# Head mixing on parts of TensorE's array: premix on quarters, mix on row halves, ten tokens gathered to partitions 4 to 123

## The chip, the cores and the metric

One core of one Trainium2 chip runs the whole kernel. The metric is device time in microseconds, the median of repeated runs. The core's engines are TensorE (PE in the profile, its weight loads are PEld), VectorE (DVE), ScalarE (ACT), GpSimd (POOL) and SyncE (SP), which here only issues transfers. SBUF is the on-chip memory of 128 partitions, PSUM holds what TensorE writes, in banks of 512 float32 per partition.

## The reference

Attention whose heads are mixed before and after the softmax ("talking heads"), followed by a gated feed-forward layer. B = 8, H = 12 heads, S = 448 tokens, D = 64; the model width is 768, the hidden width 2048, all float32.

```python
scores = scale * q @ k.transpose(0, 1, 3, 2)
scores = einsum('bhij,hg->bgij', scores, w_pre)      # "premix" over heads
scores = scores - max(scores, axis=-1)
attn = exp(scores)
attn = attn / (sum(attn, axis=-1) + 1e-9)
attn = einsum('bhij,hg->bgij', attn, w_post)         # "mix" over heads
x = (attn @ v) as (B * S, 768)
h = x @ w_in
out = (h - tanh(h)) @ w_out
```

## The kernel before

The kernel has a short prologue, an attention loop over 180 places, and a feed-forward part (from line 865 on) that the change doesn't touch.

**Blocks and groups.** The queries of a batch are cut into blocks of 120, 120, 120 and 88 tokens, 32 blocks in all. `scores` (line 465) computes a pair of heads of one block: three products of the split operands (float32r, high and low parts) on each row half of the array, as D = 64 fills half of its rows. The results land in `sts`, with a query token on each partition. A group is ten tokens of a block (nine in the last ones); `gather` (line 492) brings its 10 x 12 rows (token, head) by one transfer to 120 partitions of a tile `t`, so that mixing over heads is a product with a 120 x 120 matrix: `wpre` is block diagonal, with `w_pre` repeated for each of the ten tokens, and `wpost` holds `w_post` in an order that sorts the result by head, then token. There are 360 groups, and place p handles groups 2p and 2p + 1.

**A place** (lines 817 to 860). The order of instructions on each engine is the order in which they are written; `in_order` at the end pins it. In place p stand, one after another:

1. the copy of the previous mix result from PSUM to `at` (line 565, ScalarE),
2. the gathers for groups 2p + 4 and 2p + 5 and up to six other transfers, on SP's queue,
3. `premix(p)` (line 507): the even group as one float32 product; the odd group as three float32r products of `wph`, `wpl` (the split of `wpre`) with `th`, `tl`,
4. `norm(p - 1)`: the reciprocal of the softmax sums (VectorE) and the scaling of `wpost` by them into `wr` (line 544, ScalarE),
5. `split(2p + 3)` (line 498): the high part `th` on VectorE (line 503), the low part `tl` on GpSimd (line 504),
6. `expo(p)`: for each of the two groups the row maximum (line 526, VectorE) and the exponential with its sum (line 528, ScalarE),
7. jobs that a planner spreads over the places: transposes of k (line 415) and q (line 441), `values` (line 585, the product with v on column halves of the array, with lines 597 and 615), `scores` of a later block; their copies from PSUM follow,
8. `mix(p - 1)` (line 547): for each of the two groups and each of four chunks of 112 keys one float32 product, with the exponentials as weights (112 columns) and `wr` (120 columns) as the moving operand,
9. a step of the conversion of the feed-forward weights (lines 71 to 110, on VectorE, ScalarE and GpSimd).

The PSUM tiles are two for premix (`ps_p`), one pair of banks for mix (`ps_o`) and four for the jobs (`ps_m`). The gather tiles are two rings, of three for even groups and two for odd ones. In the prologue `wpre` and `wpost` are built from w_pre and w_post by a product with a selection matrix, copies, and selects on GpSimd that cut the block diagonal (lines 674 to 695). A float32 product shows as two records in TensorE's rows, a float32r product as one.

Of the kernel before, what the change touches and what calls it, by code (L numbers as in the profile page):

```python
# [21 lines left out]
def raw(ap):  # L22

    return ap.bitcast(F32)
# [124 lines left out]
def kernel_body(  # L149
# [11 lines left out]
    nc = tc.nc  # L161
    B, H, S, D = q.shape
    P = 128
# [3 lines left out]
    CP = 112  # L167
    NC = S // CP
    GI = P // H
    MT = GI * H  # L170
    GP = GI * H
    starts = list(range(0, S, MT))
    sizes = [min(MT, S - s) for s in starts]
    NM = len(sizes)
    scale = 1.0 / float(D) ** 0.5
# [161 lines left out]
    with ExitStack() as st:  # L337
# [17 lines left out]
        kks, vts, krs, qrs, qbs, sts, ats = {}, {}, {}, {}, {}, {}, {}  # L355
# [131 lines left out]
        tokens = {t: range(g, sizes[blocks[i][1]], ngs[blocks[i][1]]) for t, (i, g) in enumerate(groups)}  # L487
        rows = {t: H * len(x) for t, x in tokens.items()}
        at_of = {t: sum(rows[u] for u in range(t - g, t)) // H for t, (i, g) in enumerate(groups)}
        tg, ts, te = {}, {}, {}  # L490

        def gather(t, eng=nc.sync):
            i, g = groups[t]
            x = gp.tile([GP, S], F32, name="t", tag=f"t{t % 2}", bufs=3 - t % 2)
            eng.dma_start(x[: rows[t], :], sts[i][tokens[t].start : tokens[t].stop : tokens[t].step])
            tg[t] = x

        def split(t, eng=nc.gpsimd):
            n = rows[t]
            x = tg.pop(t)  # L500
            th = gp.tile([GP, S], F32R, name="th", tag="th", bufs=2)
            tl = gp.tile([GP, S], F32R, name="tl", tag="tl", bufs=2)
            nc.vector.tensor_copy(th[:n, :], x[:n, :])  # L503
            eng.tensor_sub(tl[:n, :], x[:n, :], raw(th[:n, :]))  # L504
            ts[t] = (th, tl)

        def premix(p):

            pa, pb = [ps_p.tile([P, S], F32, name="ps_p", tag="ps_p") for _ in range(2)]
            n = rows[2 * p]  # L510
            nc.tensor.matmul(pa[:n, :], wpre[:n, :n], tg.pop(2 * p)[:n, :], start=True, stop=True)  # L511
            n = rows[2 * p + 1]
            th, tl = ts.pop(2 * p + 1)
            nc.tensor.matmul(pb[:n, :], wph[:n, :n], th[:n, :], start=True, stop=False)  # L514
            nc.tensor.matmul(pb[:n, :], wpl[:n, :n], th[:n, :], start=False, stop=False)  # L515
            nc.tensor.matmul(pb[:n, :], wph[:n, :n], tl[:n, :], start=False, stop=True)  # L516
            return pa, pb

        def expo(p, pss):
            zs = gp.tile([GP, 3, 2], F32, name="zs", tag="zs")  # L520
            es = []
            for j, ps in enumerate(pss):
                n = rows[2 * p + j]

                mx = gp.tile([GP, 1], F32, name="mx", tag="mx")
                nc.vector.tensor_reduce(out=mx[:n, :], in_=ps[:n, :], axis=AX.X, op=ALU.max, negate=True)  # L526
                e = gp.tile([GP, S], F32, name="e", tag="e", bufs=4)
                nc.scalar.activation(  # L528
                    e[:n, :], ps[:n, :], AF.Exp, bias=mx[:n, :], scale=1.0, accum_out=zs[:n, 0, j : j + 1]
                )  # L530
                es.append(e)
            te[p] = [es, zs]

        def norm(p):
            zs = te[p][1]
            wr = gp.tile([GP, 2, P], F32, name="wr", tag="wr", bufs=2)[:, :, :GP]
            n0, n1 = rows[2 * p], rows[2 * p + 1]
            for j, n in enumerate((n0, n1)):

                nc.vector.tensor_scalar_add(zs[:n, 1, j : j + 1], zs[:n, 0, j : j + 1], 1e-9)  # L540
            for js, n in ((slice(0, 2), n0),) if n0 == n1 else ((slice(0, 1), n0), (slice(1, 2), n1)):
                nc.vector.reciprocal(zs[:n, 2, js], zs[:n, 1, js])
            for j, n in enumerate((n0, n1)):
                nc.scalar.mul(wr[:n, j, :], wpost[:n, :], zs[:n, 2, j : j + 1])  # L544
            te[p].append(wr)

        def mix(p):
            es, _, wr = te.pop(p)
            ps = ps_o.tile([P, 2, 512], F32, name="ps_o", tag="ps_o")
            for j, e in enumerate(es):  # L550
                i, g = groups[2 * p + j]
                n = rows[2 * p + j]
                if g == 0:
                    ats[i] = kp.tile([CP, NC, H, MT], F32, name="at", tag="at", bufs=2)
                for c in range(NC):
                    nc.tensor.matmul(  # L556
                        ps[:CP, j, c * GP : (c + 1) * GP], e[:n, c * CP : (c + 1) * CP], wr[:n, j, :],
                        start=True, stop=True,
                    )

            def rest():
                (i0, _), (i1, _) = groups[2 * p], groups[2 * p + 1]
                n0, n1, at = rows[2 * p] // H, rows[2 * p + 1] // H, at_of[2 * p]
                if i0 == i1 and n0 == n1 == GI:
                    nc.scalar.copy(  # L565
                        ats[i0][:, :, :, at : at + 2 * GI].rearrange("p c h (j i) -> p j (c h) i", j=2),
                        ps[:CP, :, : NC * GP].rearrange("p j (x i) -> p j x i", i=GI),
                    )
                    return
                for j, (i, n) in enumerate(((i0, n0), (i1, n1))):  # L570
                    at = at_of[2 * p + j]
                    nc.scalar.copy(
                        ats[i][:, :, :, at : at + n],
                        ps[:CP, j, : NC * GP].rearrange("p (c h i) -> p c h i", c=NC, i=GI)[:, :, :, :n],
                    )

            return rest
# [69 lines left out]
        now()  # L647
        load_q(2)
        now()
        tmp_w = kp.tile([P, 2 * GP + 2 * H], F32, name="tmp_w", tag="at", bufs=2)  # L650
        w12 = tmp_w[:H, 2 * GP : 2 * GP + 2 * H].rearrange("p (w h) -> p w h", w=2)
        nc.scalar.dma_start(w12[:, 0, :], w_pre)
        nc.scalar.dma_start(w12[:, 1, :], w_post)

# [5 lines left out]
        def bank():  # L660
            return ps_p.tile([P, S], F32, name="ps_p", tag="ps_p")

        def scores_of(i, hq):
# [7 lines left out]
        prep_q(0, 1)  # L671
        flush()

        repeat = tmp_w[:H, GP : 2 * GP]
        nc.gpsimd.memset(repeat, 0.0)
        nc.gpsimd.affine_select(
            out=repeat.rearrange("p (i h) -> p i h", i=GI), in_=repeat.rearrange("p (i h) -> p i h", i=GI),
            compare_op=ALU.not_equal, fill=1.0, base=0, pattern=[[0, GI], [-1, H]], channel_multiplier=1,
        )
        ps_w = bank()[:GP, : 2 * H].rearrange("p (w g) -> p w g", w=2)  # L680
        nc.tensor.matmul(ps_w.rearrange("p w g -> p (w g)"), repeat, w12.rearrange("p w g -> p (w g)"), start=True, stop=True)
        wpre, wpost = [cst.tile([GP, P], F32, name=x)[:, :GP] for x in ("wpre", "wpost")]
        pre_v = wpre.rearrange("p (i g) -> p i g", i=GI)
        post_v = wpost.rearrange("p (g i) -> p g i", i=GI)
        nc.vector.tensor_copy(pre_v, ps_w[:, 0, :].unsqueeze(1).to_broadcast([GP, GI, H]))
        nc.vector.tensor_copy(post_v, ps_w[:, 1, :].unsqueeze(2).to_broadcast([GP, H, GI]))
        for x, step in ((pre_v, [[H, GI], [0, H]]), (post_v, [[0, H], [H, GI]])):

            nc.gpsimd.affine_select(
                out=x, in_=x, compare_op=ALU.is_ge, fill=0.0, base=0, pattern=[[-a, n] for a, n in step],  # L690
                channel_multiplier=1,
            )
            nc.gpsimd.affine_select(
                out=x, in_=x, compare_op=ALU.is_ge, fill=0.0, base=H - 1, pattern=step, channel_multiplier=-1,
            )


        busy(3, ps_b)
# [17 lines left out]
        prep_q(1, 0)  # L716
        prep_q(1, 1)
        flush()
        wph, wpl = [cst.tile([GP, P], F32R, name=x)[:, :GP] for x in ("wph", "wpl")]
        nc.vector.tensor_copy(wph, wpre)  # L720
        nc.vector.tensor_sub(wpl, wpre, raw(wph))

        NG = len(groups)
        for t in range(4):
            gather(t, (nc.sync, nc.scalar)[t % 2])
        place[0] += 1
        scores_of(1, 0)
        split(1, nc.vector)
        NPL = NG // 2
        conv = Steps(narrow_steps(nc, cv, partial(dma, to=slow), chunks), 11 * len(chunks) + 1, NPL - 16)  # L730

# [85 lines left out]
        for p in range(NPL + 3):  # L817
# [15 lines left out]
            if p == NPL:  # L833
                for f in x0[1:]:
                    f()
            if p + 1 < NPL:
                split(2 * p + 3)
            if p < NPL:
                expo(p, ps)
            for f, *a in todo[p]:  # L840
# [94 lines left out]
```

## Time and profile before

| what | value |
|---|---|
| median of 3 runs | 1862.28 us (1861.75 to 1863.77) |
| the profiled execution | 1859.88 us, its span 1858.2 us |
| attention loop | 24.5 to 914 us of the span |
| TensorE busy | 1844.0 us, 99% of the span |
| VectorE, ScalarE, GpSimd busy | 1230.1, 1099.2, 455.4 us |
| granted TensorE clock | 1.00 |

The span runs from the first to the last instruction; the execution's own time is 1.7 us more. A row of a group of instructions gives the line, the engine, the operation, the tiles (out<-in) with partitions x elements, the count, the busy time and the mean duration of one; behind the bar the idle time before them and what ended it. Rows of TensorE such as 120*112 120x120 give rows*columns of the weights and the moving operand. Matmuls are pipelined: a record lasts longer than the step from one to the next.

### The profile page before, as it was taken

The page shows a single profiled execution, that of the slowest core. Times are in us where ns is not written, and L with a number is a line of the kernel's source. Part 1 is how long each engine was busy: PE and PEld are TensorE (multiplying, and loading weights), DVE is VectorE, ACT ScalarE, POOL GpSimd, SP SyncE. Part 2 cuts the span into 40 slices and gives each one's busy share as a digit, 9 for nine tenths or more (in the row PEclk, how much of TensorE's full clock was granted, in tenths as well). Part 3 has the DMA queues.
Part 4 walks back from the last instruction along what each step waited for, and adds up shares of the span by engine and source line. Part 5 has one row for each costly group of instructions (what it writes and reads, how often), then busy time and mean ns, then how long its engine had stood idle before and what let it go on. Part 6 is the DMA issues. An engine that isn't in the chain of part 4 may idle for free.

```text
span 1858.2 us, 35351 instructions
## 1 busy us (share of the span) xinstructions
PE 1844.0 (99%) x13150; PEld 1523.0 (82%) x13150; DVE 1230.1 (66%) x2549; ACT 1099.2 (59%) x2411; POOL 455.4 (25%) x401
## 2 busy tenths in 40 slices
PE   8999999999999999999999999999999999999998
PEld 6888788788888888887788888888888888888887
DVE  5787777877787777776456556565565556556555
ACT  5877878788787887877633434434444443443433
POOL 2444445444444445444200000000000000000000
PEclk9999999999999999999999999999999999999999
DMA  8668576675765758554575665655656655655651
GB/s 179 189 185 217 167 204 197 195 220 172 225 188 169 229 180 229 178 176 151 194 297 198 224 219 196 236 202 209 231 197 218 223 207 209 218 219 194 225 202 37
DMA packets 232795, 371.92 MB, mean 200 GB/s; under 512 B 98992, under 2 KB 207536, under 8 KB 218288
## 3 DMA queue, kind: packets, MB, share of 16 engines
q1 hardware_dynamic: 231740, 368.45, 61.1%
q8 instruction: 104, 1.70, 0.4%
q10 hardware_dynamic: 884, 1.22, 0.2%
q14 instruction: 67, 0.55, 0.1%
HBM read 245.37 MB, written 47.19 MB: 157 GB/s over the span
## 4 chain that ended last, share of the span: by engine, by line
PE 95%; DMA 2%; ACT 1%; DVE 1%; issue 1%; POOL 0%; SPq 0%; ACTq 0%; POOLq 0%
PE ps_o L556 17%; PE ps_m L597 8%; PE ps_h L256 8%; PE ps_h L260 8%; PE ps_h L255 8%; PE ps_p L511 7%; PE ps_q L475 7%; PE ya L303 5%; PE ya L300 5%; PE ya L301 5%; PE yb L303 3%; PE yb L301 3%; PE yb L300 3%; PE ps_p L516 2%; PE ps_p L514 2%; PE ps_p L515 2%
## 5 line engine op out<-in xcount | busy, mean ns | idle before, releaser
L556 PEld LDWEIGHTS ps_o<-wr,e 120*112 120x112 f32 (+1 forms) x2880 | 307.2, 177 | 45.9 <-issue 29.0
L556 PE MATMUL ps_o<-wr,e 120*112 120x120 f32 (+1 forms) x2880 | 340.0, 271 | 1.6 <-ACT wr L544 1.6
L504 POOL TENSOR_TENSOR tl<-t,th 120x448 fp32r<-120x448 f32 x179 | 204.6, 1143 | 378.9 <-DVE th L503 194.0
L287 ACT CAST gh<-r 128x512 fp32r<-128x512 f32 x112 | 69.6, 621 | 374.4 <-DVE r L280 374.4
L526 DVE TENSOR_REDUCE mx<-ps_p 120x1 f32<-120x448 f32 x360 | 217.7, 621 | 105.9 <-PE ps_p L511 105.6
L256 PE MATMUL ps_h<-xl,w 128*128 128x512 f32 x672 | 263.2, 392 | 0.5 <-POOL pad L222 0.5
L255 PE MATMUL ps_h<-xh,w 128*128 128x512 f32 x672 | 262.8, 391 | 0.0
L528 ACT ACTIVATE e<-ps_p,mx 120x448 f32<-120x448 f32 x360 | 225.0, 631 | 27.9 <-DVE mx L526 26.9
L245 POOL TENSOR_TENSOR xl<-rx,xh 128x512 fp32r<-128x512 f32 x38 | 56.2, 1479 | 738.7 <-ACT xh L244 723.1
L565 ACT COPY at<-ps_o 112x960 f32<-112x960 f32 x156 | 153.6, 985 | 134.1 <-PE ps_o L556 133.0
L276 DVE SCALAR_TENSOR_TENSOR r<-qa,ps_h 128x512 f32<-128x512 f32 x112 | 77.0, 688 | 158.7 <-ACT t L273 158.7
L303 PE MATMUL ya<-w,gl 128*128 128x512 f32 x448 | 176.8, 395 | 0.7 <-DVE gl L288 0.7
L300 PE MATMUL ya<-w,gh 128*128 128x512 f32 x448 | 174.9, 390 | 1.9 <-ACT gh L287 1.9
L301 PE MATMUL ya<-w,gh 128*128 128x512 f32 x448 | 174.8, 390 | 0.0
L260 PE MATMUL ps_h<-xh,w 128*128 128x512 f32 x672 | 170.5, 389 | 0.0
L511 PE MATMUL ps_p<-t,wpre 120*120 120x448 f32 x360 | 165.3, 541 | 1.7 <-ACT e L528 0.9
L597 PE MATMUL ps_m<-at,vr 112*64 112x120 f32 (+1 forms) x3072 | 161.1, 261 | 0.0
L597 PEld LDWEIGHTS ps_m<-at,vr 112*64 112x64 f32 x3072 | 147.6, 137 | 12.9 <-issue 3.3
L270 ACT ACTIVATE u<-ps_h 128x512 f32<-128x512 f32 x112 | 66.9, 597 | 149.9 <-PE ps_h L260 149.9
L260 PEld LDWEIGHTS ps_h<-xh,w 128*128 128x128 f32 x672 | 126.1, 188 | 26.2
L256 PEld LDWEIGHTS ps_h<-xl,w 128*128 128x128 f32 x672 | 126.6, 188 | 24.6 <-POOL pad L222 0.9
L255 PEld LDWEIGHTS ps_h<-xh,w 128*128 128x128 f32 x672 | 126.6, 188 | 22.9
(102 smaller groups left out, 3623.9 us busy)
## 6 DMA issues: line engine op xcount, KB each, us to landing
w<-ws SPq DMA_DIRECT2D x112, 1536.0 KB
t<-s SPq DMA_DIRECT2D x342, 210.0 KB
cr<-in_moe_w_in_dram SPq DMA_DIRECT2D x24, 512.0 KB
cr<-in_moe_w_out_dram SPq DMA_DIRECT2D x32, 384.0 KB
vr<-in_v_dram SPq DMA_DIRECT2D x24, 448.0 KB
kr<-in_k_dram SPq DMA_DIRECT2D x23, 448.0 KB
out_dram<-ob SPq DMA_DIRECT2D x24, 384.0 KB
qr<-in_q_dram SPq DMA_DIRECT2D x23, 360.0 KB
```

What stands on the lines that cost most here:

```text
L255: nc.tensor.matmul(ph, wh[:, fs], xh, start=(c == 0), stop=False)
L256: nc.tensor.matmul(ph, wh[:, fs], xl, start=False, stop=False)
L260: nc.tensor.matmul(ph, wl[:, fs], xh, start=False, stop=(c == NK - 1))
L300: nc.tensor.matmul(y, gh[:, tok], wh[:, es], start=first, stop=False)
L301: nc.tensor.matmul(y, gh[:, tok], wl[:, es], start=False, stop=False)
L303: nc.tensor.matmul(y, gl[:, tok], wh[:, es], start=False, stop=last)
L504: eng.tensor_sub(tl[:n, :], x[:n, :], raw(th[:n, :]))
L511: nc.tensor.matmul(pa[:n, :], wpre[:n, :n], tg.pop(2 * p)[:n, :], start=True, stop=True)
L526: nc.vector.tensor_reduce(out=mx[:n, :], in_=ps[:n, :], axis=AX.X, op=ALU.max, negate=True)
L528: nc.scalar.activation(e[:n, :], ps[:n, :], AF.Exp, bias=mx[:n, :], scale=1.0, accum_out=zs[:n, 0, j : j + 1])
L556: nc.tensor.matmul(ps[:CP, j, c * GP : (c + 1) * GP], e[:n, c * CP : (c + 1) * CP], wr[:n, j, :], start=True, stop=True,)
L597: nc.tensor.matmul(pv[j * D : (j + 1) * D, r, :n], vt[:, j, c, :], ats[i][:, c, 2 * hp + j, :n], start=(c == 0), stop=(c == NC - 1),)
```

## The change

Each place still handles two groups, premixed and mixed as before, but both groups go through parts of the array.

- **Gather.** One transfer per group, as before, but to partitions 4 to 123 of one of six tiles, so that five tokens (60 rows) lie on partitions 4 to 63 and five on 64 to 123. Partitions 0 to 3 of each tile are set to zero once.
- **Premix.** `wpre` becomes 128 x 64, with a block diagonal of five tokens for each row half (60 columns used, 4 zero). Four float32 products, one for each group (column half of the array and half of the PSUM tile) and each half of its tokens (row half of the array, one PSUM tile each). The split of odd groups, `th`, `tl`, `wph`, `wpl` and their instructions go.
- **Softmax.** Each of the two tiles now has the first or second five tokens of both groups, on 128 partitions.
- **Norm and mix.** `wr` has 60 columns in place of 120. Mix is 16 products in place of 8: 60 rows on one row half of the array, 112 weight columns, 60 moving columns; each writes five of every ten columns of the result. The copy behind it is the same.
- **Prologue.** The matrices are built for two positions each: four selects for the selection matrix, two products, four copies, eight selects and two sums.

```diff
+    GH = GI // 2
+    HP = GH * H
...
+        def half_rows(t):
+
+            n = rows[t] // H
+            return (GH, n - GH)
...
+        RT = 6
+        tq = [gp.tile([P, S], F32, name="t", tag=f"t{n}", bufs=1) for n in range(RT)]
+        for x in tq:
+
+            nc.gpsimd.memset(x[: D - HP, :], 0.0)
 
         def gather(t, eng=nc.sync):
             i, g = groups[t]
-            x = gp.tile([GP, S], F32, name="t", tag=f"t{t % 2}", bufs=3 - t % 2)
-            eng.dma_start(x[: rows[t], :], sts[i][tokens[t].start : tokens[t].stop : tokens[t].step])
+            x = tq[t % RT]
+            eng.dma_start(x[D - HP : D - HP + rows[t], :], sts[i][tokens[t].start : tokens[t].stop : tokens[t].step])
             tg[t] = x
 
-        def split(t, eng=nc.gpsimd):
...
         def premix(p):
...
-            pa, pb = [ps_p.tile([P, S], F32, name="ps_p", tag="ps_p") for _ in range(2)]
-            n = rows[2 * p]
-            nc.tensor.matmul(pa[:n, :], wpre[:n, :n], tg.pop(2 * p)[:n, :], start=True, stop=True)
-            n = rows[2 * p + 1]
-            th, tl = ts.pop(2 * p + 1)
-            nc.tensor.matmul(pb[:n, :], wph[:n, :n], th[:n, :], start=True, stop=False)
-            nc.tensor.matmul(pb[:n, :], wpl[:n, :n], th[:n, :], start=False, stop=False)
-            nc.tensor.matmul(pb[:n, :], wph[:n, :n], tl[:n, :], start=False, stop=True)
-            return pa, pb
+
+            pss = [ps_p.tile([P, S], F32, name="ps_p", tag="ps_p") for _ in halves]
+            ts = [tg.pop(2 * p + j) for j in range(2)]
+            for j in (1, 0):
+                for r in (1, 0):
+                    k = slice(r * D, D + r * H * half_rows(2 * p + j)[r])
+                    nc.tensor.matmul(pss[r][halves[j], :], wpre[k, :], ts[j][k, :], start=True, stop=True)
+            return pss
...
+            wr = gp.tile([P, 2, D], F32, name="wr", tag="wr", bufs=2)[:, :, :HP]
...
+            for r in range(2):
+                nc.scalar.mul(wr[:, r, :], wpost[:, :HP], zs[:, 2, r : r + 1])
             te[p].append(wr)
...
+            for r, e in enumerate(es):
                 for c in range(NC):
-                    nc.tensor.matmul(
-                        ps[:CP, j, c * GP : (c + 1) * GP], e[:n, c * CP : (c + 1) * CP], wr[:n, j, :],
-                        start=True, stop=True,
-                    )
+                    for j, a in enumerate(halves):
+                        k = slice(a.start, a.start + H * half_rows(2 * p + j)[r])
+                        nc.tensor.matmul(
+                            ps[:CP, j, c * GP : (c + 1) * GP].rearrange("p (h i) -> p h i", i=GI)[:, :, r * GH : (r + 1) * GH],
+                            e[k, c * CP : (c + 1) * CP], wr[k, r, :],
+                            start=True, stop=True,
+                        )
...
+        both = tmp_w[:, 2 * P : 2 * P + 4 * HP].rearrange("p (w a n) -> p w a n", w=2, a=2)
+        for w in range(2):
+            for a in range(2):
...
+                nc.vector.tensor_copy(x, of)
+
+                nc.gpsimd.affine_select(
...
+                nc.gpsimd.affine_select(
...
+        for w, x in enumerate((wpre, wpost)):
+            nc.gpsimd.memset(x[:, HP:], 0.0)
+            nc.vector.tensor_add(x[:, :HP], both[:, w, 0], both[:, w, 1])
...
-        wph, wpl = [cst.tile([GP, P], F32R, name=x)[:, :GP] for x in ("wph", "wpl")]
-        nc.vector.tensor_copy(wph, wpre)
-        nc.vector.tensor_sub(wpl, wpre, raw(wph))
...
-        split(1, nc.vector)
...
-            if p + 1 < NPL:
-                split(2 * p + 3)
```

More of the change, by code (lines that the diff above doesn't have):

```diff
@@ L489, in kernel_body @@
         at_of = {t: sum(rows[u] for u in range(t - g, t)) // H for t, (i, g) in enumerate(groups)}
-        tg, ts, te = {}, {}, {}
+        tg, te = {}, {}
+        def half_rows(t):
[5 more added lines that the diff above has]
+            nc.gpsimd.memset(x[: D - HP, :], 0.0)
         def gather(t, eng=nc.sync):
             i, g = groups[t]
-            x = gp.tile([GP, S], F32, name="t", tag=f"t{t % 2}", bufs=3 - t % 2)
-            eng.dma_start(x[: rows[t], :], sts[i][tokens[t].start : tokens[t].stop : tokens[t].step])
+            x = tq[t % RT]
+            eng.dma_start(x[D - HP : D - HP + rows[t], :], sts[i][tokens[t].start : tokens[t].stop : tokens[t].step])
@@ L496, in gather @@
             tg[t] = x
-        def split(t, eng=nc.gpsimd):
[L499 to L505, printed above, removed]
-        def premix(p):
-            pa, pb = [ps_p.tile([P, S], F32, name="ps_p", tag="ps_p") for _ in range(2)]
-            n = rows[2 * p]
-            nc.tensor.matmul(pa[:n, :], wpre[:n, :n], tg.pop(2 * p)[:n, :], start=True, stop=True)
-            n = rows[2 * p + 1]
-            th, tl = ts.pop(2 * p + 1)
-            nc.tensor.matmul(pb[:n, :], wph[:n, :n], th[:n, :], start=True, stop=False)
-            nc.tensor.matmul(pb[:n, :], wpl[:n, :n], th[:n, :], start=False, stop=False)
-            nc.tensor.matmul(pb[:n, :], wph[:n, :n], tl[:n, :], start=False, stop=True)
-            return pa, pb
+        def premix(p):
+            pss = [ps_p.tile([P, S], F32, name="ps_p", tag="ps_p") for _ in halves]
[5 more added lines that the diff above has]
+            return pss
@@ L519, in expo @@
         def expo(p, pss):
-            zs = gp.tile([GP, 3, 2], F32, name="zs", tag="zs")
+            zs = gp.tile([P, 3, 2], F32, name="zs", tag="zs")
             es = []
[L522 to L529, printed above, removed]
-                )
+            for r, ps in enumerate(pss):
+                mx = gp.tile([P, 1], F32, name="mx", tag="mx")
+                nc.vector.tensor_reduce(out=mx, in_=ps, axis=AX.X, op=ALU.max, negate=True)
+                e = gp.tile([P, S], F32, name="e", tag="e", bufs=4)
+                nc.scalar.activation(e, ps, AF.Exp, bias=mx, scale=1.0, accum_out=zs[:, 0, r : r + 1])
@@ L535, in norm @@
             zs = te[p][1]
[L536 to L544, printed above, removed]
+            wr = gp.tile([P, 2, D], F32, name="wr", tag="wr", bufs=2)[:, :, :HP]
+            for r in range(2):
+                nc.vector.tensor_scalar_add(zs[:, 1, r : r + 1], zs[:, 0, r : r + 1], 1e-9)
+            nc.vector.reciprocal(zs[:, 2], zs[:, 1])
+            for r in range(2):
+                nc.scalar.mul(wr[:, r, :], wpost[:, :HP], zs[:, 2, r : r + 1])
             te[p].append(wr)
@@ L549, in mix @@
             ps = ps_o.tile([P, 2, 512], F32, name="ps_o", tag="ps_o")
-            for j, e in enumerate(es):
+            for j in range(2):
                 i, g = groups[2 * p + j]
-                n = rows[2 * p + j]
                 if g == 0:
                     ats[i] = kp.tile([CP, NC, H, MT], F32, name="at", tag="at", bufs=2)
+            for r, e in enumerate(es):
                 for c in range(NC):
-                    nc.tensor.matmul(
-                        ps[:CP, j, c * GP : (c + 1) * GP], e[:n, c * CP : (c + 1) * CP], wr[:n, j, :],
-                        start=True, stop=True,
-                    )
+                    for j, a in enumerate(halves):
[5 more added lines that the diff above has]
+                        )
             def rest():
@@ L649, in kernel_body @@
         now()
-        tmp_w = kp.tile([P, 2 * GP + 2 * H], F32, name="tmp_w", tag="at", bufs=2)
-        w12 = tmp_w[:H, 2 * GP : 2 * GP + 2 * H].rearrange("p (w h) -> p w h", w=2)
+        tmp_w = kp.tile([P, 2 * P + 4 * HP + 2 * H], F32, name="tmp_w", tag="at", bufs=2)
+        w12 = tmp_w[:H, 2 * P + 4 * HP :].rearrange("p (w h) -> p w h", w=2)
         nc.scalar.dma_start(w12[:, 0, :], w_pre)
@@ L672, in kernel_body @@
         flush()
-        repeat = tmp_w[:H, GP : 2 * GP]
+        AT = ((D - HP, D), (0, D))
+        repeat = tmp_w[:H, : 2 * P].rearrange("p (w m) -> p w m", w=2)
         nc.gpsimd.memset(repeat, 0.0)
[L676 to L695, printed above, removed]
+        ps_w = bank()[:, : 2 * H].rearrange("p (w g) -> p w g", w=2)
@@ new lines, in kernel_body @@
+        for w in range(2):
+            for at in AT[w]:
+                x = repeat[:, w, at : at + HP].rearrange("p (i h) -> p i h", i=GH)
+                nc.gpsimd.affine_select(
+                    out=x, in_=x, compare_op=ALU.not_equal, fill=1.0, base=0, pattern=[[0, GH], [-1, H]],
+                    channel_multiplier=1,
+                )
+            nc.tensor.matmul(ps_w[:, w, :], repeat[:, w, :], w12[:, w, :], start=True, stop=True)
+        wpre, wpost = [cst.tile([P, D], F32, name=x) for x in ("wpre", "wpost")]
@@ new lines, in kernel_body @@
+        both = tmp_w[:, 2 * P : 2 * P + 4 * HP].rearrange("p (w a n) -> p w a n", w=2, a=2)
+        for w in range(2):
+            for a in range(2):
+                if w == 0:
+                    x = both[:, w, a].rearrange("p (i g) -> p i g", i=GH)
+                    of, step = ps_w[:, w, :].unsqueeze(1).to_broadcast([P, GH, H]), [[H, GH], [0, H]]
+                else:
+                    x = both[:, w, a].rearrange("p (g i) -> p g i", i=GH)
+                    of, step = ps_w[:, w, :].unsqueeze(2).to_broadcast([P, H, GH]), [[0, H], [H, GH]]
+                nc.vector.tensor_copy(x, of)
+                nc.gpsimd.affine_select(
+                    out=x, in_=x, compare_op=ALU.is_ge, fill=0.0, base=-AT[w][a], pattern=[[-m, n] for m, n in step],
+                    channel_multiplier=1,
+                )
+                nc.gpsimd.affine_select(
+                    out=x, in_=x, compare_op=ALU.is_ge, fill=0.0, base=AT[w][a] + H - 1, pattern=step,
+                    channel_multiplier=-1,
+                )
```

## The prediction

> **What bounds the kernel now.** I read the page's busy shares and its chain of what ended last first, then the busy time by stretches, then the chain in order of time around 500 us, where every step of the attention loop has its own line.
>
> ```profile
> span 1858.2 us, 35351 instructions
> PE 1844.0 (99%) x13150; PEld 1523.0 (82%) x13150; DVE 1230.1 (66%) x2549; ACT 1099.2 (59%) x2411; POOL 455.4 (25%) x401
> PE 95%; DMA 2%; ACT 1%; DVE 1%; issue 1%; POOL 0%; SPq 0%; ACTq 0%; POOLq 0%
> ```
>
> TensorE is busy all the time and makes 95% of the chain. The stretches (span, then busy time and instructions of each engine, clock, DMA share, GB/s):
>
> ```profile
> 24.50:914.00 889.50, 887.55 (x8192) 712.24 (x8192) 672.93 (x1732) 702.60 (x1735) 396.56 (x349) 1.00 0.65 194
> 499.17:503.78 4.61, 4.61 (x36) 3.47 (x35) 3.41 (x10) 4.42 (x11) 1.83 (x2) 1.00 1.04 308
> 510.34:514.95 4.61, 4.61 (x35) 3.49 (x34) 3.80 (x7) 3.67 (x9) 1.15 (x1) 1.00 0.74 239
> ```
>
> The first row is the attention loop, 180 places in 889.5 us; the diff touches nothing after it. Two places with scores follow: TensorE is full in both, but ScalarE (fourth number) already has 4.42 and 3.67 of 4.61 us. It is the next limit. The chain through two places (start, length, step, records):
>
> ```profile
> 499.33 0.75 PE ps_p L511 x2
> 500.08 0.20 PE ps_p L514
> 500.29 0.20 PE ps_p L515
> 500.49 0.21 PE ps_p L516
> 500.70 1.42 PE ps_q L475 x12
> 502.12 1.82 PE ps_o L556 x16
> 503.94 0.75 PE ps_p L511 x2
> 504.69 0.20 PE ps_p L514
> 504.90 0.20 PE ps_p L515
> 505.10 0.20 PE ps_p L516
> 505.30 0.77 PE ps_m L415 x8
> 506.07 2.61 PE ps_m L597 x48
> ```
>
> So premix takes 1.36 us (0.75 for the float32 group, whose product makes two records of 0.375, and three times 0.20 for the split one), scores 1.42, transposes 0.77, values 2.61, mix 1.82. A switch of the array's shape shows in it: within mix one record follows the other after 0.1025 us (next fence), 16 of them are 1.64, so 0.18 us are lost ahead of it after scores; the 24 pairs of values at the same pace are 2.46, so 0.15 are lost there; transposes, which follow premix on the full array, lose nothing.
>
> ```profile
> 502.05 0.36 PE L556 MATMUL ps_o<-wr,e 120*112 120x120 f32 x1
> 502.05 1.89 PE L556 MATMUL ps_o<-wr,e 120*112 120x120 f32 x16
> 506.00 0.32 PE L597 MATMUL ps_m<-at,vr 112*64 112x120 f32 x2
> 506.00 2.68 PE L597 MATMUL ps_m<-at,vr 112*64 112x120 f32 x48
> 501.13 0.37 PE L475 MATMUL ps_q<-kk,ql 64*120 64x448 f32 x2
> 502.04 0.27 PEld L556 LDWEIGHTS ps_o<-wr,e 120*112 120x112 f32 x2 [0.32 <-issue]
> 500.94 0.18 PEld L475 LDWEIGHTS ps_q<-kk,ql 64*120 64x120 f32 x2
> 506.00 0.14 PEld L597 LDWEIGHTS ps_m<-at,vr 112*64 112x64 f32 x2
> L556 PEld LDWEIGHTS ps_o<-wr,e x2880: 172/177/179, 32.0 to 916.3; 120*112 120x112 f32 x184, 108*112 108x112 f32 x8
> ```
>
> These rows are from narrow windows of the timeline. Mix: the first record ends 0.36 after its start, all 16 after 1.89, so 15 steps of 0.102. Values: two records together take 0.32, and 48 take 2.68, so (2.68-0.32)/23 = 0.1026 per pair: column halves run two products at once, in float32, although each product is a high and a low record. Scores: two records in 0.37 us on row halves, at once too. Loads of weights: two in a row on the full array take 0.27, one 0.177, so the second starts 0.095 after the first: 112 columns occupy the load path for 0.095 us. Two for row halves (0.18) or column halves (0.14) take as long as one: they don't queue.
>
> **The change, part by part.**
>
> *Premix* becomes four float32 products, one on each quarter of the array, each 2 records of 448 columns. No row shows quarters. Lower bound: all four at once, 2 x 0.375 = 0.75 us. Upper bound: two at once, as halves are shown to run, 1.50; none at once would be 3.00. I take 0.75, because column halves and row halves each run at once here with moving data of their own, and the four write two PSUM tiles as the scores do. That is 0.61 less per place, x180 = **-110**.
>
> *Mix* becomes 16 float32 products of 60 rows, 112 weight columns and 60 moving columns, that is 16 records on each row half. Streaming needs half of 0.102, 0.051; loading the 112 columns 0.095 as before, since the scores' loads of 64 rows take what loads of 120 rows do. Lower bound of a step 0.051 (loads free), upper 0.146 (each load after the half's stream). On the full array both lie over each other (0.095 of load and 0.10 of stream in 0.102), so I take the load alone with a little on top, 0.097: 16 x 0.0055 less, x180 = **-16**. The strided output (5 of every 10 columns) has no row; even at twice the stream it would hide under the load.
>
> Here the page "TensorE: Matmul & The Clock Gate" of the Trainium skill (Part 3, What overlaps and what doesn't) speaks against the change: a weight load overlaps a matmul in flight only where the row group differs. Mix before disagrees, 0.102 us where load and stream one after the other would be 0.195. By the rule mix would lose, not gain; that is the third rival.
>
> *Switches.* I price one by the three above: 0.15 into 64 columns, 0.18 to 0.20 into more; bounds 0 and 0.20. Counts of places come from records:
>
> ```profile
> L597 PE MATMUL ps_m<-at,vr 112*64 112x120 f32 (+1 forms) x3072 | 161.1, 261 | 0.0
> L475 PE MATMUL ps_q<-kk,qh 64*120 64x448 f32 (+1 forms) x768 | 118.6, 385 | 0.9 <-ACT kk L426 0.4 <-ACT qh L454 0.3 <-DVE kk L427 0.2
> L475 PE MATMUL ps_q<-kk,ql 64*120 64x448 f32 (+1 forms) x384 | 70.7, 363 | 0.0
> L441 PE MATMUL ps_m<-ident,qr 120*128 120x120 f32 (+1 forms) x186 | 22.8, 258 | 0.0
> L415 PE MATMUL ps_m<-ident,kr 112*128 112x112 f32 x168 | 19.5, 258 | 0.0
> ```
>
> Scores: 1152/12 = 96, four of them before the loop: 92. Values: 3072/48 = 64, two after the last premix: 62. Transposes: 168/8 + 186/6 - 1 = 51, of which 40 stand in a place with values and 11 alone; 180-92-62-11 = 15 places have premix and mix only. New: mix to premix 180 x 0.15 = +27; premix to transposes or straight to mix 66 x 0.19 = +12.5; transposes alone to mix 11 x 0.18 = +2. Saved: scores to mix, now of one shape, 92 x 0.18 = -16.6. Sum **+25**. With this TensorE alone comes to -110-16+25 = -101 us.
>
> *Removed:* the split, and the two products of weights.
>
> ```profile
> L504 POOL TENSOR_TENSOR tl<-t,th 120x448 fp32r<-120x448 f32 x179 | 204.6, 1143 | 378.9 <-DVE th L503 194.0
> L544 ACT ACTIVATE wr<-wpost,zs 120x120 f32<-120x120 f32 x344 | 117.6, 393 | 1.6 <-DVE zs L542 1.0
> L528 ACT ACTIVATE e<-ps_p,mx 120x448 f32<-120x448 f32 x360 | 225.0, 631 | 27.9 <-DVE mx L526 26.9
> SPq L495 <- PE ps_p L516: 281.9, 123, 5.8
> ```
>
> The split lay off the chain, so I cost its removal at nothing; it frees GpSimd and VectorE. The gathers (as many, as large, same place on SP's queue) wait as now for the premix of the place before and have until two places later; SP's wait for that premix (last row) grows shorter with it.
>
> *Where TensorE is no longer last.* (a) Places with scores: 4.60-0.61-0.09+0.15-0.18 = 3.87 us of TensorE. ScalarE: the mean of 4.42 and 3.67 is 4.05; the two products for wr shrink from 120 to 60 columns, and by the rows above (448 columns 631 ns, 120 columns some 340 of a pair of 680) that is about 0.05 each, so 3.94. Exponentials also start later against the end of premix, as both tiles are now complete at the same moment. I take 3.97, +0.1 x 92 = **+9**. (b) The 15 bare places:
>
> ```profile
> 33.94 0.98 ACT L565 COPY at<-ps_o 112x960 f32<-112x960 f32 x1 [0.75 <-PE ps_o L556]
> 34.81 0.68 ACT L544 ACTIVATE wr<-wpost,zs 120x120 f32<-120x120 f32 x2
> 35.26 1.89 PE L556 MATMUL ps_o<-wr,e 120*112 120x120 f32 x16
> ```
>
> Mix starts there when wr's first half is done, after the copy of the previous result, so a shorter premix is not felt: they gain 0.1, not 0.36, **+4**. (c) Ahead of the loop, wpre and wpost each need two selects per half and a sum on VectorE that waits for GpSimd; behind it in VectorE's order stands L427:
>
> ```profile
> 9.50 0.35 POOL L689 TENSOR_SCALAR_AFFINE_SELECT wpre<-wpre 120x120 f32<-120x120 f32 x1 [7.53 <-DVE wpre L685]
> 11.29 1.16 DVE L427 TENSOR_TENSOR kk<-ps_k,kk 128x448 fp32r<-128x448 f32 x2 [1.67 <-ACT kk L426]
> ```
>
> Eight selects from 9.50 at 0.36 end at 12.4, so L427 and the scores behind it come some 1.2 us late; the first place, which loses its wait for the split, gives part back: **+1** (bounds 0 and 1.5). The memsets of six gather tiles lie in GpSimd's 7.53 us of idle time.
>
> **Sum.** -101+9+4+1 = -87 us. The profiled execution took 1859.88 us, 1.7 around its span, so 1773; the median of the runs shown, 1862.28, is 2.4 above it, 1775 on that scale. I predict 1774, between the two.
>
> **Rivals.** *ScalarE sets the pace in places with scores* (13%). For it: 4.42 in one of the two rows, and a strict order in which score copies stand behind the exponentials. Against: scores mostly alternate with places of 6.56 us where it has slack to catch up. At 4.31 (4.42 less 0.11) instead of 3.97 it adds 0.34 x 92 = 31: 1805.
>
> *Quarters run only two at a time* (10%), slower than before. For it: no row shows four. Premix is then 1.50, +0.75 x 180 = 135 against TensorE's -101, and ScalarE's terms vanish: +34, 1894. It turns from gain to loss where premix takes about 1.31 us.
>
> *A half's load waits for that half's stream* (5%): a step of mix is 0.146 instead of 0.097, +0.049 x 16 x 180 = 141: -101+141 = +40, 1900. Against: 0.102 per step now.
>
> *Loads of both halves queue after all* (1%): 32 x 0.095 = 3.04 per mix, +1.49 x 180 = 268: 2040. The 0.18 for two loads speaks against it.
>
> **Numbers.** 68% for my forecast, whose own range is 1757 to 1791: a switch 0.05 us cheaper or dearer (180+66+11 come, 92 go: 165 x 0.05 = 8) and term (a) from 0 to twice (9). The last 3% are for something I don't see, 1 faster and 2 without change. The range 1740 to 1840 takes in the first rival with a score place up to 0.4 us worse, and at the low end new switches for nothing (25 less: 1749) with a mix step of 0.094; it leaves out the three slow rivals, 16%. A measurement here can't tell less than 0.2% from no change. Faster 68+13+1 = 82%, same 2%, slower 10+5+1 = 16%.
>
> **What would show it.** Premix as 8 records of which four start within some 20 ns, 0.75 us in the chain; if they start in two rounds, the second rival holds. Mix as 32 records at about 0.097 per pair; 0.146 means the third. Gaps of 0.15 before each premix. Places with scores near 3.9 to 4.0, bare ones near 3.2. ScalarE busy some 86% of a loop of about 800 us, with TensorE waiting for e at premix (L511 before) if the first rival holds. I am wrong if the loop does not get shorter than 850 us.

## The result and the profile after

| | before | after |
|---|---|---|
| median of 4 runs | 1862.01 us | 1793.99 us (1788.66 to 1800.72) |
| span of the profiled execution | 1858.2 us | 1786.9 us |
| first premix to last premix | 24.5 to 910.0 us | 25.8 to 839.7 us |
| mean granted clock | 1.000 | 0.992 |

The ratio is 0.9635, with a 95% interval of 0.9602 to 0.9669: 68 us less, where 87 were forecast. 1794 is 20 us above the 1774 forecast, 3 above the upper end of the forecast's own range (1757 to 1791), and inside the wider range of 1740 to 1840. The changed kernel also spreads more from run to run, 12 us against 2. The page of the changed kernel, its busy shares, the chain by engine and the groups that answer to those of before:

```profile
span 1786.9 us, 41553 instructions
PE 1750.8 (98%) x16572; PEld 1425.8 (80%) x16572; DVE 1125.4 (63%) x2362; ACT 1082.3 (61%) x2411; POOL 253.7 (14%) x237
PE 83%; ACT 6%; DMA 5%; DVE 2%; issue 2%; SPq 1%; POOL 0%; ACTq 0%; DVEq 0%; POOLq 0%
L559 PE MATMUL ps_o<-wr,e 60*112 60x60 f32 (+1 forms) x5760 | 316.9, 260 | 14.2 <-ACT wr L544 14.2
L521 PE MATMUL ps_p<-t,wpre 60*64 60x448 f32 (+1 forms) x1440 | 180.1, 569 | 2.8 <-DMA t<-s 2.7
```

Premix is now L521, mix L559. TensorE still leads, but the chain is only 83% its own instead of 95%: ScalarE and transfers have entered it. A place with scores and the premix behind it, from the chain in order of time (start, length, step, records):

```profile
443.13 0.91 PE ps_p L521 x8
444.05 1.41 PE ps_q L477 x12
445.46 1.53 PE ps_o L559 x32
446.99 0.91 PE ps_p L521 x8
```

Such a place was 4.60 us and is 3.85: premix went from 1.36 to 0.91, which includes 0.16 for the switch ahead of it; mix from 1.82 to 1.53, now without a switch, as it has the shape of the scores. These are the steps as forecast. What is missing is elsewhere. The stretches of the loop (span, TensorE's busy time and records, clock, DMA share, GB/s):

```profile
24.50:840.00 815.50, 790.73 (x11560) 0.99 0.72 210
108.00:112.00 4.00, 2.63 (x44) 0.95 0.88 221
112.00:116.00 4.00, 4.00 (x34) 0.63 0.51 187
116.00:120.00 4.00, 4.00 (x62) 1.00 0.50 156
312.00:316.00 4.00, 2.73 (x42) 1.00 0.98 222
316.00:320.00 4.00, 3.98 (x40) 0.55 0.92 296
320.00:324.00 4.00, 4.00 (x36) 0.60 0.53 169
324.00:328.00 4.00, 4.00 (x64) 1.00 0.30 109
```

In the whole loop TensorE has 24.8 us without work, where it had 2.0 before. Who ended its waits (line, for what, us in total, times, longest):

```profile
PE ps_o L559 <- ACT wr L544: 14.2, 23, 1.4
PE ps_m L601 <- ACT at L569: 4.3, 4, 2.9
PE ps_m L601 <- ACT at L576: 3.5, 5, 1.0
PE ps_p L521 <- DMA t<-s: 2.7, 4, 1.6
PE ps_m L601 <- DMA vr<-in_v_dram: 1.7, 2, 1.1
```

Without the waits ahead of the first premix (1.6 of the fourth row) and behind the last (1.8 of the first), ScalarE ended 20.2 us of them and transfers 2.8. That doesn't say why ScalarE was late; one case below begins with a late load.

And behind a stretch with a gap the granted clock falls to 0.55 to 0.63 in rows of 4 us: TensorE is then busy, but slowly. Windows cut to these stretches show that it was exactly half clock, for 3.41 or 6.83 us at a time:

```profile
111.57:114.98 3.41, 3.41 (x20) 0.50 0.55 200
316.37:323.20 6.83, 6.83 (x54) 0.50 0.79 258
725.97:732.80 6.83, 6.83 (x52) 0.50 0.57 201
```

To size this I took the start of each premix as the start of a place, sorted the places by the jobs in them, and called the length that the undisturbed ones of a kind share (the 15th percentile) their clean length; what a place takes beyond it is its **excess**. Before, the 180 places sum to 888.8 us with 2.2 of excess, so 886.6 clean. After, 817.2 with 33.0, so 784.2 clean. The clean places gained 102.4 us; the excess took back 31. The excess of a kernel is that of its one profiled execution, so a few us of difference between two kernels can be the spread of their runs.

### The profile page after: what moved, and what is told of

It is laid out like the page before. It is cut to its first block, busy times and chain, and to the rows that moved or that the text cites. A ratio compares the mean times of both kernels' runs of the same rounds, so it can differ in the third digit from the quotient of the medians.

```text
span 1786.9 us, 41553 instructions
## 1 busy us (share of the span) xinstructions
PE 1750.8 (98%) x16572; PEld 1425.8 (80%) x16572; DVE 1125.4 (63%) x2362; ACT 1082.3 (61%) x2411; POOL 253.7 (14%) x237
## 4 chain that ended last, share of the span: by engine, by line
PE 83%; ACT 6%; DMA 5%; DVE 2%; issue 2%; SPq 1%; POOL 0%; ACTq 0%; DVEq 0%; POOLq 0%
PE ps_o L559 12%; PE ps_h L257 8%; PE ps_h L258 8%; PE ps_h L262 8%; PE ps_m L601 8%; PE ps_p L521 7%; PE ya L305 6%; PE ya L302 6%; PE ya L303 6%; PE ps_q L477 5%; PE yb L305 3%; PE yb L303 3%; PE yb L302 3%; DMA t<-s 2%; ACT e L532 2%
## 5 line engine op out<-in xcount | busy, mean ns | idle before, releaser
L559 PEld LDWEIGHTS ps_o<-wr,e 60*112 60x112 f32 (+1 forms) x5760 | 306.8, 176 | 44.8 <-ACT wr L544 30.3
L559 PE MATMUL ps_o<-wr,e 60*112 60x60 f32 (+1 forms) x5760 | 316.9, 260 | 14.2 <-ACT wr L544 14.2
L530 DVE TENSOR_REDUCE mx<-ps_p 128x1 f32<-128x448 f32 x360 | 207.6, 619 | 157.2 <-PE ps_p L521 157.1
L532 ACT ACTIVATE e<-ps_p,mx 128x448 f32<-128x448 f32 x360 | 226.0, 637 | 25.7 <-DVE mx L530 25.2
L521 PE MATMUL ps_p<-t,wpre 60*64 60x448 f32 (+1 forms) x1440 | 180.1, 569 | 2.8 <-DMA t<-s 2.7
L277 DVE TENSOR_SCALAR far<-u 128x512 f32<-128x512 f32 x112 | 47.9, 428 | 140.5 <-ACT u L272 134.8
```

The costliest lines, as they stand in the source:

```text
L521: nc.tensor.matmul(pss[r][halves[j], :], wpre[k, :], ts[j][k, :], start=True, stop=True)
L530: nc.vector.tensor_reduce(out=mx, in_=ps, axis=AX.X, op=ALU.max, negate=True)
L532: nc.scalar.activation(e, ps, AF.Exp, bias=mx, scale=1.0, accum_out=zs[:, 0, r : r + 1])
L559: nc.tensor.matmul(ps[:CP, j, c * GP : (c + 1) * GP].rearrange("p (h i) -> p h i", i=GI)[:, :, r * GH : (r + 1) * GH], e[k, c * CP : (c + ...
```

## The experiments

Theory 1: ScalarE comes late in some places, TensorE idles, and idle time costs clock behind it. Theory 2: transfers come late. Theory 3: the denser use of the array costs clock by itself. All expectations speak of these; the first four have theories 1 and 2 under one name, "Theory", and mostly theory 3 as rival 2.

**The two products for wr on VectorE**

```diff
-                nc.scalar.mul(wr[:, r, :], wpost[:, :HP], zs[:, 2, r : r + 1])
+                nc.vector.tensor_scalar_mul(wr[:, r, :], wpost[:, :HP], zs[:, 2, r : r + 1])
```

> The two products for wr run on VectorE instead of ScalarE; nothing else changes. The changed kernel takes 1794 us, 20 more than the forecast; its places exceed their clean lengths by 33 us in all, 23 of them TensorE idle, and its mean granted clock is 0.992 instead of 1.000. Theory (ScalarE comes late in bare places and the places behind them, and idle time then costs clock): the 7 us of excess in bare places and some of the 10 in score places go, about 1784 us, clock above 0.994. Rival 1 (only late transfers make the idle time): 1794, no change. Rival 2 (the denser use of the array costs clock, whatever the idle time): clock stays at 0.992 and no more than 4 us are gained.

Measured: 1801.5 us, 0.9682 (0.9666 to 0.9698), clock 0.994, excess 42 us. A miss for theory 1: nothing is gained, and the median is 7 us above that of the changed kernel, though the two intervals just touch. Theory 3, which allowed no gain above 4 us, isn't refuted by it. The waits of weight loads, first of the changed kernel, then of this one (line, for what, us in total, times, longest):

```profile
PEld ps_o L559 <- ACT wr L544: 30.3, 33, 2.1
```

```profile
PEld ps_o L559 <- ACT at L569: 28.5, 27, 2.6
```

The wait for wr is gone, and as long a one for line 569 stands in its place: ScalarE's copy of the previous mix result, which must empty the one PSUM tile before mix may write it again. ScalarE was late before it came to wr, so taking wr off it frees nothing at that point. The three shortest bare places do get shorter (2.87 to 2.92 us, where the shortest were 3.10), but the median of the 14 grows from 3.24 to 3.57, and the excess in all by 9 us, more than half of it in places with transposes and values. VectorE has 96 us more to do; that it delays others there is likely, but was not shown.

**Fewer transfers at a time, later conversion**

```diff
-            if not landed(1):
+            if not landed(3):
...
-            issue(6)
+            issue(2)
```

> At most two loads or stores per place stand behind the gathers instead of six, and a loaded weight chunk is converted three places after its load was issued instead of one. Theory (both ScalarE and late transfers make idle time): the excess of places with k transposes and values, 8 us, and of values alone, 5 us, shrinks, about 1785 us. Rival 1 (only late transfers matter): 1774, clock 1.00. Rival that ScalarE alone matters: 1794. Rival 2 (density costs clock): clock stays at 0.992.

Measured: 1819.7 us, 0.9777 (0.9762 to 0.9793), clock 0.984. Another miss, but of two parts. The excess of places with transposes and values falls from 8.4 to 0.8 us: in the changed kernel the largest of them began with this (chain, start, length):

```profile
45.19 8.52 DMA cr<-in_moe_w_in_dram
53.71 0.02 issue
53.73 0.44 DVE cm L80
54.17 0.02 issue
54.20 0.63 ACT cm L82
54.83 0.87 ACT at L569
```

A weight chunk landed late, VectorE and then ScalarE stood before the conversion of it, and the copy of a mix result and TensorE's values stood behind them. That is mended. But the conversion now falls behind, and what is left of it runs in one piece near the end of the loop (stretch with all engines: TensorE 3.23 us busy of 15, VectorE 12.57, GpSimd 10.65, clock 0.76):

```profile
835.00:850.00 15.00, 3.23 (x56) 2.45 (x48) 12.57 (x18) 5.45 (x11) 10.65 (x11) 0.76 0.41 133
```

That one place has 18.7 of the 51.5 us of excess, and the clock stands at 0.50 from 842.84 us on for 34 us. Without that place there would be 33 as in the changed kernel, so even then nothing was won in the sum: other places lost what these gained.

**Both**

> Both edits. Theory: about 1775 us, near the forecast, idle time of the loop under 8 us and a clock of 0.998 or more. Rival 2 (density costs clock): clock 0.992 again, 1785 us or more.

Measured: 1826.3 us, 0.9809 (0.9791 to 0.9828), excess 61 us, clock 0.982. It fails as its parts do, and it can't tell theory 3 from the others, since it adds idle time instead of taking it away.

**Bare places filled**

```diff
             for f, *a in todo[p]:
                 f(*a)
+            if 1 <= p < NPL and not any(f in rank for f, *a in todo[p]):
+                busy(2, ps_m.tile([P, 512], F32, name="ps_b", tag="ps_m"))
```

> In the 14 bare places two products of the identity (0.43 us and a switch of shape, results unused) are added on TensorE between premix and mix, where it waits for wr. Theory (idle time costs clock in the following places): bare places get no shorter, but the score places behind them keep the full clock, which now lose 1.5 to 2 us each at three of them; about 1789 us, clock 0.994 or more. Rival 2 (density costs clock): clock 0.992 or less, 1794 to 1800 us.

Measured: 1788.9 us, 0.9614 (0.9600 to 0.9628), clock 0.994. The time is as expected, with bare places 0.17 us longer where nothing was late, though the interval overlaps that of the changed kernel. In the trace, the bare place near 104 us keeps a gap of 0.73 us instead of 1.37, and the score place behind it runs at its clean length instead of 1.57 us over; the same holds near 310 and 724 us (2.0 and 1.8 us over before). More work on TensorE made the following places quicker, which theory 3 has no room for.

**Conversion steps on GpSimd**

```diff
-    nc.scalar.mul(m, m, 2.0**-112)
+    nc.gpsimd.tensor_scalar_mul(m, m, 2.0**-112)
...
-    nc.scalar.copy(fh, m)
+    nc.gpsimd.tensor_copy(fh, m)
```

> Two of the three ScalarE steps of the weight conversion (lines 82 and 102, 56 times each, 0.54 to 0.65 us) move to GpSimd, which the change left idle for 86% of the span; 66 us less on ScalarE. In the trace of the changed kernel the chains into the longer bare places and places with transposes and values run through these steps. Theory 1 (ScalarE lag makes most of the 33 us of excess): excess falls to about 20 us, and with less idle time the clock rises to 0.995 or more; 1780 us, against 1794. Theory 2 (late transfers make most of it): 1790 to 1794. Theory 3 (the denser array costs clock): clock 0.992, 1788 or more.

Measured: 1782.5 us, 0.9581 (0.9554 to 0.9608), excess 21.7 us, clock 0.994 (0.989 to 0.995 in the four runs). Near theory 1 in time (1780) and in excess (20), below its 0.995 of clock. ScalarE's busy time fell by 45 us, not by 66. So some 11 us of the 31 went with a part of ScalarE's load; the interval of this kernel and that of the changed one (from 0.9602 on) still overlap by a hair.

**Bulk transfers on a queue of their own**

```diff
-                    send(x, nc.sync)
+                    send(x, nc.gpsimd)
```

> In the loop the bulk loads and stores are issued from GpSimd, on a queue of their own; the gathers stay on SP's queue and no longer stand behind them. In the changed kernel one gather took 8.9 us to land and held premix, and five of the longer places follow late gathers or late loads. Theory 2 (late transfers): those waits go, excess falls from 33 to about 20 us, 1782 us. Theory 1 (ScalarE lag): 1792 or more, since the bare places stay as they are; issuing may delay GpSimd's part of the conversion.

Measured: 1834.6 us, 0.9830 (0.9786 to 0.9875), excess 81 us, clock 0.973. Theory 2 expected the late gathers to go. The longest landing of a gather in the chain of the changed kernel was the first of these rows, here it is the second:

```profile
163.75 8.89 DMA t<-s
```

```profile
595.14 17.84 DMA t<-s
```

So late transfers do cost time, theory 2 is right on that, but a queue of its own is no cure. TensorE's idle time that a gather ended rose from 2.7 to 17.3 us. The DMA share was 0.95 to 1.07 from 588 to 604 us and 0.68 to 1.01 in the rows below, so the DMA engines were full, or nearly so, for most of that gather's time. That the order on the one queue had protected the gathers, and that another queue gives them no place ahead of the rest, is my reading of it, not shown apart; GpSimd's busy time also rose, from 254 to 439 us, with the issuing, and what that delayed was not separated. While this gather was under way TensorE waited 4.20 us, up to 606.30, for an earlier gather, and that gap cost clock too (span, TensorE busy, clock, DMA share, GB/s):

```profile
602.00:604.00 2.00, 0.11 (x3) 0.98 0.98 253
604.00:606.00 2.00, 0.00 (x0) 0.50 0.75 211
606.00:608.00 2.00, 1.70 (x8) 0.50 0.96 238
608.00:610.00 2.00, 2.00 (x14) 0.50 1.01 305
610.00:612.00 2.00, 2.00 (x36) 0.81 0.68 204
```

**Both moves**

> Both edits. If the two causes add: excess near 10 us, clock 0.998, about 1770 us, which is the forecast. If the clock loss belongs to the denser array: clock still 0.992 and 1782 or more.

Measured: 1816.6 us, 0.9764 (0.9729 to 0.9799), excess 50, clock 0.988, far from the 1770 hoped for. It lies between its parts: the conversion steps give about 18 us here, the queue takes some 34.

**Premix issued twice**

```diff
-            for j in (1, 0):
-                for r in (1, 0):
+            for j, r in [(j, r) for _ in range(2) for j in (1, 0) for r in (1, 0)]:
+                if True:
```

> The four premix products are issued twice in a row, to the same results. It measures what premix costs without the switch of shape ahead of it. Four quarters at once: +2 x 0.375 = 0.75 us per place on TensorE, 16 records in 1.66 us in the chain, at most +135 us in all, less what other waits hide: 1900 to 1930. Two at a time: +1.50 per place, 2040 or more.

Measured (one run): 1895.6 us, a little below the expected 1900; span 1893.9, clock 0.998. The chain:

```profile
446.44 1.66 PE ps_p L521 x16
448.10 1.38 PE ps_q L477 x12
449.48 1.53 PE ps_o L559 x32
```

1.66 as expected for four quarters at once: the second round costs 0.75 us, the switch 0.16. The clean lengths sum to 128 us more (0.75 in 166 places, but 0.28 in the 14 bare ones, where TensorE had waited), the loop rises by 105 only, because the excess falls from 33.0 to 9.4. That is the strongest evidence of the set: the same transfers and the same ScalarE work in longer places leave hardly any gap. Behind the first premix and up to the last, ScalarE ended 1.7 us of TensorE's waits instead of 20.2, and transfers none. With more work on quarters the clock rises: there are two stretches of half clock, one behind the 1.64 us gap ahead of the first premix and one behind the loop, and from 30.22 to 951.82 us it is 1.00. Theory 3 falls.

**Mix not in turn**

```diff
-                for c in range(NC):
-                    for j, a in enumerate(halves):
+                for j, a in enumerate(halves):
+                    for c in range(NC):
```

> Within mix, the four products of one row half are issued before the four of the other, instead of in turn; nothing else. If a product on one half starts past waiting ones of the other half (as the pairs of values, written high, low, high, low, were read): mix stays at 1.53 us behind scores and the time at 1789 to 1800. If products start strictly in the order written: the halves no longer overlap but at the borders, mix takes about 32 x 0.095 = 3.0 us, and the time is 2030 or more.

Measured (one run): 1860.5 us, span 1858.8. The chain through such a place:

```profile
452.88 0.91 PE ps_p L521 x8
453.80 1.41 PE ps_q L477 x12
455.21 2.07 PE ps_o L559 x32
```

Neither expectation holds: mix takes 2.07 us, not 1.53 and not 3.0. The other half's products do start ahead of waiting ones, but only some four records ahead, so that the first and the last four or so of the 32 run alone, 0.10 us apart (starts at 455.10, 455.20, 455.30, 455.40 and at 456.73, 456.83, 456.92, 457.02). The 0.54 us more per place are 97 us, the loop rose by 70 only, as the excess fell from 33.0 to less than 5: longer places hide the delays again, as with premix issued twice.

**Combinations**

The next three add to the conversion steps on GpSimd: the fill; smaller bursts (`issue(3)`, and `NPL - 24` in place of `NPL - 16`, so that the conversion ends earlier); and both.

> The two conversion steps on GpSimd (which alone gave 1783) and the two filling products in bare places (which alone gave 1789 against 1794). If the two gains come from different idle time (ScalarE lag; idle time that is turned into clock loss): 1776 to 1779. If the fill only helped through the same bare places that the conversion step already mended: 1782.

> The two conversion steps on GpSimd, at most three bulk transfers per place instead of six, and the conversion paced to end eight places earlier, so that nothing of it is left for one place as in the kernel with two transfers per place. If late gathers and loads behind bursts are the rest of the excess (21.7 us in the kernel with the conversion steps alone): 1770 to 1775. If the order of the transfers doesn't matter, because the DMA engines are full for the time: 1782, or more with the quicker conversion.

> Conversion steps on GpSimd, fill, smaller bursts. If all add: about 1768 to 1772. If only the first counts: 1782.

| added to the conversion steps | median | ratio, 95% interval | excess | clock |
|---|---|---|---|---|
| nothing | 1782.5 us | 0.9581 (0.9554 to 0.9608) | 21.7 us | 0.994 |
| the fill | 1780.2 us | 0.9561 (0.9534 to 0.9588) | 15.1 us | 0.996 |
| smaller bursts | 1777.1 us | 0.9549 (0.9531 to 0.9568) | 20.1 us | 0.995 |
| both | 1779.0 us | 0.9561 (0.9510 to 0.9612) | 17.4 us | 0.995 |

The intervals overlap, so these don't rank; what they add to the conversion steps alone is at most a few us and not settled. None reached the time that was expected if the gains add (1776 to 1779, 1770 to 1775, 1768 to 1772). The ones with the fill and with smaller bursts lie clear of the changed kernel (0.9602 at the lowest); the latter beats both kernels, at 1777 us, by 17 and 85 us.

## Why the prediction was right, and where it was off

**Premix on quarters** held: 0.75 us for four quarters at once, -110. The second rival is out: the chain has 0.91 with the switch, and twice the work adds 0.75.

**Mix** held: 32 records in 1.53 us behind scores, 0.096 a pair, where 0.097 was taken as the load's own time; -16 was forecast, (1.64-1.53) x 180 = 20 came. The rule of the Trainium skill weighed there ("TensorE: Matmul & The Clock Gate", Part 3, What overlaps and what doesn't) doesn't hold for this kernel: a half's load lies over that half's stream, or a pair would take 0.146. That rival and the one of queued loads are out.

**Switches** held: 0.16 into premix, 1.72 for mix behind values against 1.53 behind scores, so 0.19, and none between scores and mix.

Together: TensorE's sum of -101, with the bare places' +4 a clean -97, was measured as -102.4.

**Prologue**: the first premix starts at 25.8 instead of 24.5 us, +1.3 against +1.

**Where TensorE is no longer last, (a)** is the term that was mis-sized. It was 9 us for ScalarE's load, in score places alone; the excess took 31, over all kinds of places. I had named the engine and let it cost a uniform 0.1 us per score place. In fact clean score places reach TensorE's 3.85, ScalarE's mean is no bound on them, and the loss comes in some thirty single places, where ScalarE is late (conversion steps, score copies, the copy of line 569, wr, in a row) or a gather or load lands late. By kind, score places have 10.2 of the 33.0, against 1.6 before; that the growth is near 9 is luck, as 5.8 of it is half clock, in three score places that each follow a bare place with a gap. The rest had no term: 7.0 in bare places, 13.6 in places with values (8.4 of it where transposes of k stand with them), 2.1 in places with transposes of k alone. The first rival had ScalarE as the uniform pace of score places; its 1805 is not what happened either.

**What no term had** is the clock. The span has 27.3 us at half clock, with TensorE busy all through, so 13.7 us were lost by it. Of these 1.7 lie behind the loop and 1.7 in the first place; 10.2 are in the excess of 33.0, not quite a third. The other 23 are left to the waits. I had carried the 1.00 of the old kernel over, whose TensorE never waited.

Sum: -102.4 clean, +30.8 excess, +1.3 prologue, -1.0 after the loop is -71.3, the difference of the two spans.

## What to carry to other kernels

Where one engine is full, the others may be late by as much as its work in a place covers; shorten that work, and delays that were hidden come out one by one, not as a mean. So size the second engine by its heaviest places and their order of work, and look at the transfers in bursts. And where TensorE will newly have gaps of a microsecond or more, allow for the clock that may follow them: here about a third of what was lost.

## What was not expected of the hardware

**Short gaps can cost clock.** Single gaps of TensorE of 1.37 us (ahead of 109.88), 1.28 (316.02) and 1.17 (725.83) were each followed by 3.4 or 6.8 us at half clock; one of 1.15 us (422.41) was not, and gaps up to 0.7 us never were in the bare places looked at:

```profile
109.88 1.78 PE L559 MATMUL ps_o<-wr,e 60*112 60x60 f32 x32 [1.37 <-ACT wr L544]
111.60 1.77 PE L521 MATMUL ps_p<-t,wpre 60*64 60x448 f32 x8
113.30 1.10 PE L477 MATMUL ps_q<-kk,qh 64*120 64x448 f32 x4
422.41 1.78 PE L559 MATMUL ps_o<-wr,e 60*112 60x60 f32 x32 [1.15 <-ACT wr L544]
424.12 0.98 PE L521 MATMUL ps_p<-t,wpre 60*64 60x448 f32 x8
```

Premix takes 1.77 us behind the first gap and 0.98 behind the last. The Trainium skill ("TensorE: Matmul & The Clock Gate", Why this matters for your kernels) warns of gaps above about 3 us; here less than half of that was enough. The length of a gap alone doesn't decide it: in the kernel with all three additions a gap of 2.01 us (ahead of 263.75) was not followed by half clock, and one of 1.00 (ahead of 106.88) was. What the trace of the changed kernel does show is a grid. Its stretches of half clock begin at 26.24, 56.96, 111.57, 316.37, 725.97 and 845.44 us, each a whole number of steps of 3.413 us behind the first (9, 25, 85, 205 and 240), and last one or two steps. So it may count how a gap lies to these steps; what exactly decides is open.

**A product passes waiting ones of another part of the array, but not far.** Four records ahead or so in mix, 2.07 us instead of 1.53. In this kernel the parts had to be issued in turn.
